# One written order for the steps of the first four pairs of heads

## The chip, the cores and the metric

The kernel runs on one core of a Trainium2 chip. The metric is the device time of one execution in microseconds (us); the time before is 978.82 us, the median of three runs (978.48 to 979.66).

## The reference

Attention over 4 batches of 8 heads with 576 positions of 64 values, in float32, then two feed-forward blocks over the 2304 tokens of 512 values:

```python
q_rot, k_rot = rotate(q), rotate(k)                   # x1*cos - x2*sin, x1*sin + x2*cos
scores = q_rot @ k_rot.T / 8
attn = exp(scores - max(scores)); attn /= attn.sum() + 1e-9
x = (attn @ v) as [2304, 512]
x = gate * relu(x @ w1[e]) @ w2[e]                    # e = the best of 8 experts, for each token
out = relu(x @ w_in) ** 2 @ w_out
```

## The kernel before

The 32 heads are worked on as 16 pairs, 0 to 15; two heads fill the 128 partitions. A pair goes through steps, each a Python function that issues a few instructions. The change names each step by a letter; this document does so throughout, so that `S1.2` is score unit 2 of pair 1:

- **L** `load`: one DMA of q and k (1280 KB) into tile `qk`, which has two buffers. **V** `load_v`: one DMA of v (320 KB) into tile `V`, two buffers. Both are issued on SP's queue.
- **R** or **Q** `rotate`: three elementwise operations (two products, one sum), in place in `qk`, on DVE (R) or on POOL (Q). The number behind the pair is 0 for k, 1 for q, empty for both; the last number says which of the three.
- **H** `high`: ACT copies `qk` rounded to fp32r into `XH`. **W** or **w** `low`: what the rounding left goes to `XL`, on POOL (W) or DVE (w). H and W are the last readers of a `qk` buffer, so the load of two pairs later waits for them.
- **Z** `stack_up`: ten DMAs inside SBUF, on SP's queue, that stack high and low parts into `kZ`, `qZ` and `QH` (four for k, six for q). Pair 0 does without them: **b**, **c** and **d** build its parts by columns on DVE and ACT, and each of its score units is followed by two warm-up matmuls.
- **S** `scores`: one of nine score units of a pair, 4 matmuls of 288 columns (6 in unit 8) into one of two PSUM buffers `ps`. **M** `smax`: the row maximum on DVE. **X** `sexp`: the exponential on ACT, which frees the buffer.
- **U** `turn`: one of eleven transposing units, four 128x128 transposes of the exponentials on TensorE (one in unit 6), into one of four PSUM buffers `pp`. **O** `turned`: the copy out, on DVE for seven units and on ACT for four.
- **A** `values`: half of the product with v, 20 short matmul instructions that need all of the pair's O and its `V`. **G** `gathered`: its copy out. **J** `project`, **F** `finish`: the projection by identity and gate weights, and the division on DVE. **K** `gate_weights`: DMAs of the gate weights and of a table of constants.

Nothing reorders instructions: each engine runs them in the order in which the functions are called, and each DMA is issued in SP's order, so that an instruction which waits holds up what is behind it on its engine. That order comes from a heap of (time, function) pairs that `at` fills and a loop at the end of `attention` empties. For each pair, `on` adds the pair's number times 15.954 to a step's offset in `OFF`. Pair 0's score units and pair 1's rotations stand in a list, `opening()`, at times 0.0, 0.1 and so on, ahead of all offsets; `FIRST` draws six of pair 0's transposing units to times 29.5 to 30.5. So pair 0's transposes are issued after its last score unit. Pair 2 has its own branch: q rotated on POOL, k on DVE. A tile's buffer passes to the next user when the last reader of its content is done, also where that reader is issued later on another engine.

After attention come routing and the experts, with weights that are loaded during attention, and a dense block; both are long runs of matmuls.

Of the kernel before, what the change touches and what calls it, by code (L numbers as in the profile page):

```python
# [21 lines left out]
B, H, S, D = 4, 8, 576, 64  # L22
# [37 lines left out]
def shape_constants():  # L60
# [27 lines left out]
    for b in range(B):  # L88
        for c in range(4):
# [21 lines left out]
           un=[32.589, 32.153, 35.217, 38.036, 36.617, 23.748, 28.906, 37.6, 35.653, 34.253, 33.817],  # L111
           out=[33.418, 34.148, 36.917, 39.025, 37.411, 29.788, 32.958, 38.405, 36.294, 35.538, 34.643],
           av=[41.194, 44.969], x=[46.747, 47.789], pj=54.426, fin=58.03)
FIRST = [(0, 1), (0, 0), (1, 3), (1, 2), (0, 2), (1, 1)]
ON_DVE = [(0, 0), (0, 3), "LQ", "CR", (1, 0), (1, 1), (1, 3)]


def attention(tc, rope, ident, qk, v, w_gate, xd, on_batch, later, ahead):
    nc = tc.nc
# [59 lines left out]
    def warm(n):  # L179
        nc.tensor.matmul(T["warm"][:, 0:n], T["hi", 0][:, 0, 0:128], T["hi", 0][:, 0, 0:n], start=True, stop=True)  # L180

    def opening():


        two = lambda s: (lambda: scores(0, s), lambda: smax(0, s), lambda: sexp(0, s))
        S, M, X = [dict(zip(range(9), [two(s)[n] for s in range(9)])) for n in range(3)]
        step = lambda n, i: lambda: rotate(1, n, nc.vector, i)
        return [S[0], S[1], lambda: rotate(0, 1, nc.vector, cols=Z), lambda: direct_high(0, Z), M[0], X[0], M[1], X[1],
                lambda: direct_low(0, nc.vector, Z), lambda: load(2), S[4], S[5], step(0, 0), M[4], X[4], step(0, 1), M[5], X[5],
                step(0, 2), S[8], S[2], M[8], X[8], lambda: high(1, 0), lambda: low(1, 0), lambda: stack_up(1, 0),  # L190
                step(1, 0), M[2], X[2], step(1, 1), S[3], S[6], M[3], X[3], step(1, 2), lambda: high(1, 1), M[6], X[6],
                lambda: low(1, 1), lambda: stack_up(1, 1), lambda: load_v(0), S[7], M[7], X[7]]
# [26 lines left out]
    def load(P):  # L219
        t = T["qk", P] = ldp.tile([128, 2, 2, 640], F32, name="qk", tag="qk", bufs=2)  # L220
        src = qk[P].rearrange("p (w n c) -> p w n c", w=2, n=2)
        if P < 2:
            for n, c in ([(0, h) for h in HALF] + [(1, A), (1, Z)] if P == 0 else [(n, slice(0, 640)) for n in range(2)]):
                nc.sync.dma_start(out=t[:, :, n, c], in_=src[:, :, n, c])
        else:
            nc.sync.dma_start(out=t, in_=src)
# [5 lines left out]
    def rotate(P, n, eng, step=None, cols=slice(0, 640)):  # L232
        x, a = T["qk", P], slice(0, 2) if n is None else slice(n, n + 1)
        for i, (f, o, y) in enumerate(((times, 0, TB[:, 0, a, cols]), (times, 1, TB[:, 1, a, cols]), (plus, 0, x[:, 1, a, cols]))):
            if step in (None, i):
                f(eng, x[:, o, a, cols], x[:, o, a, cols], y)

    def high(P, n=None, cols=slice(0, 640)):

        if ("hi", P) not in T:  # L240
            T["hi", P] = zp.tile([128, 2, 640], F32R, name="XH", tag="XH", bufs=2)
        a = slice(0, 2) if n is None else slice(n, n + 1)
        nc.scalar.activation(T["hi", P][:, a, cols], T["qk", P][:, 0, a, cols], AF.Copy)

    def low(P, n=None, eng=None):
        if ("lo", P) not in T:
            T["lo", P] = zp.tile([128, 2, 640], F32R, name="XL", tag="XL", bufs=2)
        a = slice(0, 2) if n is None else slice(n, n + 1)
        args = T["lo", P][:, a], T["qk", P][:, 0, a], T["hi", P][:, a].bitcast(F32)
        if eng is None:  # L250
            nc.gpsimd.tensor_sub(*args)
        else:
            minus(eng, *args)
# [16 lines left out]
    def scores(P, s):  # L270

        t = T["S", P, s] = ps.tile([128, 2, 512], F32, name="ps", tag="ps", bufs=2)
        if s < 8:
            j, c = divmod(s, 4)
            todo, qs, qh = [j], slice(c * 128, c * 128 + 128), QH[P % 2][j]
            qh = qh[:, qs]
        else:
            todo, qs, qh = [0, 1], slice(512, 640), T["hi", P][:, 1, 512:640]
        k0 = 0 if s in (4, 5, 6, 7) else 64
        if P == 0:  # L280
            H, L = T["hi", P], T["lo", P]
            ql = L[:, 1, 512:640] if s == 8 else T["qZ", 2 * P + j][:, qs]
            for i, (q1, k1) in enumerate(((qh, H), (ql, H), (qh, L))):
                for u in range(2):
                    nc.tensor.matmul(t[:, u, 0:288], q1, k1[:, 0, k0 + 288 * u:k0 + 288 * u + 288], start=i == 0, stop=i == 2)
            for u in range(2):
                warm(288)
            return
        for i, j in enumerate(todo):
            Q1, K1 = T["qZ", 2 * P + j], T["kZ", 2 * P + j]  # L290
            for u in range(2):
                nc.tensor.matmul(t[:, u, 0:288], Q1[:, qs], K1[:, k0 + 288 * u:k0 + 288 * u + 288], start=i == 0, stop=False)  # L292
        for u in range(2):
            nc.tensor.matmul(t[:, u, 0:288], qh, T["lo", P][:, 0, k0 + 288 * u:k0 + 288 * u + 288], start=False, stop=True)  # L294
# [6 lines left out]
    def smax(P, s):  # L301
        nc.vector.tensor_reduce(small("mx", P, 9)[:, s:s + 1], T["S", P, s][:, :, 0:288], axis=AX.XY, op=ALU.max, negate=True)  # L302

    def sexp(P, s):
        if ("e", P) not in T:
            T["e", P] = (wp.tile([128, 4, 1152], F32, name="e", tag="e", bufs=2), wp.tile([128, 576], F32, name="e4", tag="e4", bufs=2))
        ed = T["e", P][1] if s == 8 else T["e", P][0][:, s % 4, 576 * (s // 4):576 * (s // 4) + 576]
        sc = s if s < 4 else (4 if s == 8 else s + 1)
        nc.scalar.activation(ed.rearrange("p (u n) -> p u n", u=2), T["S", P, s][:, :, 0:288], AF.Exp,  # L309
                             bias=T["mx", P][:, s:s + 1], accum_out=SS[P % 6][:, sc, 0:1])  # L310
# [87 lines left out]
            at(t, lambda: route(P, t))  # L398

    prepare()  # L400
    for n, f in enumerate(opening()):
        at(.1 * n, f)
    at(24.0, gate_weights)
    for P in range(NPAIR):
        def on(o, f, *args):
            at(OFF["pair"] * P + o, lambda: f(*args))

        if P > 2:
            on(OFF["load"], load, P)
        if P > 0:  # L410
            on(OFF["v"] + (1.8 if P == NPAIR - 1 else 0), load_v, P)
        if P > 1:
            for i in range(3):
                if P == 2:
                    on(OFF["rope"] + 2.93 * i, rotate, P, 1, nc.gpsimd, i)
                    on(1.1 + 1.35 * i, rotate, P, 0, nc.vector, i)
                else:
                    on(OFF["rope"] + 2.93 * i, rotate, P, None, nc.gpsimd, i)
            for n, hi, lo in ((1, 1.6, 1.7), (0, 4.7, 4.75)) if P == 2 else ((None, OFF["hi"], OFF["lo"]),):
                on(hi, high, P, n)  # L420
                on(lo, low, P, n)
            on(OFF["z"], stack_up, P)
        for s in range(9) if P else ():
            w = {1: 8, 8: 1}.get(s, s) if P == 1 else s
            on(OFF["S"][w], scores, P, s)
            on(OFF["max"][w], smax, P, s)
            on(OFF["exp"][w], sexp, P, s)
        for un, o, o2 in zip(UNITS, OFF["un"], OFF["out"]):
            if P == 0 and un in FIRST:
                o, o2 = [t + .2 * FIRST.index(un) for t in (29.5, 29.6)]  # L430
            on(o, turn, P, un)
            on(o2, turned, P, un)
        for u in range(2):
            on(OFF["av"][u], values, P, u)
            on(OFF["x"][u], gathered, P, u)
        on(OFF["pj"], project, P)
        on(OFF["fin"], finish, P)
        if P % 4 == 3 and P + 1 < NPAIR:
            on(OFF["fin"] + .02, route, P)
    at(OFF["pair"] * (NPAIR - 1) + OFF["lo"] + .01, swap.close)  # L440
    at(OFF["pair"] * (NPAIR - 1) + max(OFF["S"]) + .01, turned_in.close)
    ahead(lambda t, f: at(t, f), lambda: ppt("pp"))
# [845 lines left out]
```

## Time and profile before

| | |
|---|---|
| median of three runs | 978.82 us |
| the profiled execution | 982.82 us, its span 981.0 us |
| TensorE matmul (PE) busy | 961.1 us, 98% of the span |
| VectorE (DVE) / ScalarE (ACT) / GpSimd (POOL) busy | 55% / 43% / 33% |
| mean granted TensorE clock | 0.994 of 2.4 GHz |

The profile is one execution; its times count from the start of the span, and the other 1.8 us of the profiled execution lie around it. PE is the matmul engine, PEld its weight loads, SPq the queue on which SP issues DMAs. A clock of 0.50 in a row is the lower of TensorE's two levels, 1.2 GHz.

### The profile page before, as it was taken

Reading aid. Unit: us, or ns where it says so; the run is one execution under the profiler, and the core shown is the slowest. Engines: PE = TensorE matmul, PEld = TensorE weight load, DVE = VectorE, ACT = ScalarE, POOL = GpSimd, SP = SyncE. Lnnn points to the kernel's source line nnn. Section 1 sums busy time; section 2 is a strip of 40 time slices with the busy share of each in tenths; the row PEclk is TensorE's granted clock in tenths of the full one; section 3 lists DMA queues with packets and bytes.
Section 4 is the critical chain, followed back from the end, with each engine's and each line's share of the span. In section 5 each row is a group of like instructions: output and inputs, shape, how many; then the busy total and the mean of one; then the engine's idle time right before and its main releaser. Section 6 shows DMA issues by size and latency. Waiting matters only on the chain. (4 is left out here: it accounts for less than half of the span.)

```text
span 981.0 us, 15523 instructions
## 1 busy us (share of the span) xinstructions
PE 961.1 (98%) x5565; PEld 825.5 (84%) x5565; DVE 537.5 (55%) x949; ACT 422.3 (43%) x840; POOL 320.1 (33%) x261
## 2 busy tenths in 40 slices
PE   8899999999999999999999999999999999999997
PEld 7687878788787888888888789999999999999996
DVE  7677877777867355574685479522323323222222
ACT  5576757575641233352464367522322322222222
POOL 3776887887475221142354300010000100100101
PEclk9899999999999999999999999999999999999999
DMA  6876777766632823455486423100100200100000
GB/s 210 257 201 194 230 214 188 247 186 164 184 110 89 313 97 130 131 182 176 160 277 229 165 90 129 33 33 1 33 33 1 65 1 31 35 1 1 33 1 33
DMA packets 46353, 119.83 MB, mean 122 GB/s; under 512 B 8240, under 2 KB 9776, under 8 KB 43952
## 3 DMA queue, kind: packets, MB, share of 16 engines
q1 hardware_dynamic: 40752, 101.58, 33.6%
q0 software_dynamic: 4960, 16.43, 4.9%
q8 instruction: 46, 0.75, 0.3%
q10 hardware_dynamic: 544, 0.66, 0.2%
q14 instruction: 51, 0.42, 0.1%
HBM read 79.93 MB, written 15.11 MB: 97 GB/s over the span
## 5 line engine op out<-in xcount | busy, mean ns | idle before, releaser
L1114 PE MATMUL o<-Wo,gs 128*128 128x512 f32 x864 | 214.7, 393 | 0.0
L1093 PE MATMUL h<-xs,Wi 128*128 128x384 f32 x1008 | 189.6, 336 | 0.0
L1114 PEld LDWEIGHTS o<-Wo,gs 128*128 128x128 f32 x864 | 159.9, 188 | 28.7 <-DVE gs L1104 0.3
L1093 PEld LDWEIGHTS h<-xs,Wi 128*128 128x128 f32 x1008 | 178.2, 188 | 6.6
L1102 DVE SCALAR_TENSOR_TENSOR g<-h,r 128x384 f32<-128x384 f32 x80 | 44.6, 558 | 190.6 <-ACT r L1098 190.6
L309 ACT ACTIVATE e<-ps,mx 128x576 f32<-128x576 f32 x144 | 106.2, 740 | 86.8 <-DVE mx L302 86.7
L1129 POOL DMA_INDIRECT out_dram<-os,at x18 | 17.8, 987 | 369.3 <-DVE os L1124 309.9
L1098 ACT ACTIVATE r<-h 128x384 f32<-128x384 f32 x96 | 47.1, 490 | 204.6 <-PE h L1093 204.6
L302 DVE TENSOR_REDUCE mx<-ps 128x1 f32<-128x576 f32 x144 | 105.9, 753 | 53.0 <-PE ps L294 53.0
L916 PE MATMUL p_y<-W,hh 128*128 128x512 f32 x504 | 122.9, 399 | 0.8 <-ACTq L928 0.8
L887 PE MATMUL p_h<-W,xs 128*128 128x512 f32 x480 | 114.9, 394 | 0.0
L916 PEld LDWEIGHTS p_y<-W,hh 128*128 128x128 f32 x504 | 93.1, 188 | 22.2 <-ACTq L928 1.1
L887 PEld LDWEIGHTS p_h<-W,xs 128*128 128x128 f32 x480 | 88.5, 188 | 18.4 <-DVEq L928 0.7
L327 PE MATMUL pp<-ident,e 128*128 128x128 f32 x640 | 87.0, 277 | 1.6 <-DVE eT L343 1.3
L1104 DVE TENSOR_TENSOR gs<-g,gs 128x384 fp32r<-128x384 f32 x96 | 53.6, 558 | 56.0 <-ACT gs L1103 56.0
L459 POOL TENSOR_TENSOR qk<-qk,TB 128x1280 f32<-128x1280 f32 (+1 forms) x28 | 78.6, 2824 | 2.2 <-DMA qk<-in_qk_dram 2.2
L327 PEld LDWEIGHTS pp<-ident,e 128*128 128x128 f32 x640 | 75.7, 143 | 3.2 <-DVE eT L343 1.8
L292 PE MATMUL ps<-kZ,qZ 128*128 128x288 f32 x300 | 72.1, 330 | 3.9 <-ACT e L309 3.0
L1103 ACT ACTIVATE gs<-g 128x384 fp32r<-128x384 f32 x96 | 50.4, 525 | 50.5 <-DVE g L1102 50.0
L354 PE MATMUL av<-eT,V 128*64 128x288 f32 x512 | 69.1, 412 | 0.0
L343 DVE COPY eT<-pp 128x512 f32<-128x512 f32 x96 | 64.3, 684 | 5.8 <-PE pp L327 4.0
L292 PEld LDWEIGHTS ps<-kZ,qZ 128*128 128x128 f32 x300 | 45.8, 192 | 19.3 <-issue 6.7
(237 smaller groups left out, 1206.0 us busy)
## 6 DMA issues: line engine op xcount, KB each, us to landing
qk<-in_qk_dram SPq DMA_DIRECT2D x14, 1280.0 KB, 6.4
raw<-in_moe_w_dram SPq DMA_DIRECT2D x30, 512.0 KB, 5.5
kZ<-XH SPq DMA_DIRECT2D x60, 160.0 KB, 2.8
rawa<-in_moe_w_dram SPq DMA_DIRECT2D x18, 512.0 KB, 3.7
w<-in_moe_w_in_dram SPq DMA_DIRECT2D x8, 1024.0 KB, 6.0
w<-in_moe_w_out_dram SPq DMA_DIRECT2D x8, 1024.0 KB, 5.0
V<-in_v_dram SPq DMA_DIRECT2D x16, 320.0 KB, 3.0
qZ<-XH SPq DMA_DIRECT2D x30, 160.0 KB, 2.9
```

What stands on the lines that cost most here:

```text
L292: nc.tensor.matmul(t[:, u, 0:288], Q1[:, qs], K1[:, k0 + 288 * u:k0 + 288 * u + 288], start=i == 0, stop=False)
L302: nc.vector.tensor_reduce(small("mx", P, 9)[:, s:s + 1], T["S", P, s][:, :, 0:288], axis=AX.XY, op=ALU.max, negate=True)
L309: nc.scalar.activation(ed.rearrange("p (u n) -> p u n", u=2), T["S", P, s][:, :, 0:288], AF.Exp, bias=T["mx", P][:, s:s + 1], accum_out=SS ...
L327: nc.tensor.transpose(t[:, c * 128:c * 128 + 128], src, ident)
L343: nc.vector.tensor_copy(o, i)
L354: nc.tensor.matmul(t[64 * j:64 * j + 64], V[:, j, kc], eT[:, j, kc, cs] if kc < 4 else eL[:, cs], start=kc == 0, stop=kc == 4)
L459: v.tensor_tensor(out=out, in0=a, in1=b, op=ALU.mult)
L887: nc.tensor.matmul(t[u], s[:, a, k], W1[:, b, k, 512 * u:512 * u + 512], start=n == 0, stop=n == 11)
L916: nc.tensor.matmul(t, s[:, a, k], W2[:, b, k], start=n == 0, stop=n == 23)
L1093: nc.tensor.matmul(t, W[:, a, k, fs], s[:, c, k], start=n == 0, stop=n == 11)
L1104: nc.vector.tensor_sub(gs[:, 1], g, gs[:, 0].bitcast(F32))
L1114: nc.tensor.matmul(self.T["o", b][c], gs[:, a, 128 * c:128 * c + 128], W[:, w], start=(f == 0 and n == 0), stop=(f == 15 and n == 2))
```

## The change

`opening()` and `FIRST` go. In their place a string `ORDER` gives 228 steps of pairs 0 to 3, with the loads and preparation of pair 4, one after the other; step n stands at time 75.70 n / 228 on the same heap. `do` turns a token into its call. A token in `ORDER` is left out of the loop over pairs; all others keep their offsets, so steps of pairs 4 to 6 whose offset is below 75.70 fall between the written ones: `L5`, `L6`, `V4` and `Q5..0` to `Q5..2`. Behind the written stretch the heap gives out the same steps in the same order as before.

In the order that results, pair 0's transposes stand between score units of pairs 0 and 1. One low part of pair 1 is made on DVE (`w1.1`); two of pair 2's q rotations go to DVE and two of its k rotations to POOL. `K` comes early, ahead of `L2`. Around `V2` the heap gives, with pair 5's and 6's steps by their times: `H4 S3.4 ... X3.4 ... S3.1 ... Q5..0 S3.0 J1 M3.0 U2.7 L6 X3.1 X3.0 S3.5 W4 V2 Q5..1 S3.7 V4 O2.9 O2.7 Z4 M3.5 A2.0`; before, `V2` stood between `L4` and `Z3`, and `W4` ahead of `Q5..0`, `Z4` and `L6`.

```diff
--- before.py
+++ after.py
@@ -111,7 +111,17 @@
            un=[32.589, 32.153, 35.217, 38.036, 36.617, 23.748, 28.906, 37.6, 35.653, 34.253, 33.817],
            out=[33.418, 34.148, 36.917, 39.025, 37.411, 29.788, 32.958, 38.405, 36.294, 35.538, 34.643],
            av=[41.194, 44.969], x=[46.747, 47.789], pj=54.426, fin=58.03)
-FIRST = [(0, 1), (0, 0), (1, 3), (1, 2), (0, 2), (1, 1)]
+UNTIL = 75.70
+ORDER = """
+    b S0.1 M0.1 c S0.0 X0.1 d M0.0 R1.0.0 S0.4 M0.4 X0.0 S0.5 R1.0.1 M0.5 X0.4 S0.8 R1.0.2 X0.5 M0.8 K S0.2 H1.0 R1.1.0 X0.8 R1.1.1 L2 R1.1.2 S0.3 M0.2
+    H1.1 X0.2 M0.3 U0.6 w1.1 X0.3 U0.5 S0.7 W1.0 R2.1.0 M0.7 S0.6 Z1.0 Q2.1.1 U0.2 Z1.1 M0.6 R2.0.0 U0.1 X0.7 L3 S1.2 O0.2 X0.6 R2.1.2 O0.1 S1.1 M1.2 M1.1
+    U0.7 O0.6 U0.3 O0.3 X1.2 X1.1 S1.4 M1.4 U0.0 H2.1 Q2.0.1 O0.7 S1.8 Q2.0.2 M1.8 W2.1 X1.4 H2.0 O0.5 U0.10 S1.0 M1.0 X1.8 O0.0 U0.9 U0.4 S1.5 M1.5 U1.5
+    O0.4 X1.0 X1.5 O0.10 U0.8 S1.6 U1.6 O0.8 O0.9 W2.0 Q3..0 V0 S1.7 M1.6 M1.7 O1.5 Z2 X1.6 A0.0 Q3..1 Q3..2 S2.2 X1.7 U1.10 O1.6 U1.9 G0.0 U1.7 O1.9 M2.2
+    X2.2 O1.10 S1.3 M1.3 X1.3 L4 H3 A0.1 S2.8 S2.4 O1.7 U1.0 V1 M2.8 M2.4 U1.1 G0.1 X2.8 O1.0 W3 X2.4 U1.8 U1.2 O1.8 S2.1 O1.2 U1.3 Q4..0 M2.1 S2.0 J0
+    O1.1 U1.4 X2.1 O1.3 M2.0 X2.0 U2.5 O1.4 S2.7 Z3 S2.5 O2.5 M2.7 X2.7 A1.0 M2.5 F0 S2.3 X2.5 S2.6 M2.3 M2.6 X2.3 X2.6 Q4..1 A1.1 G1.1 S3.2 Q4..2 U2.1
+    M3.2 S3.8 U2.6 G1.0 M3.8 U2.0 O2.0 O2.1 X3.2 U2.3 H4 S3.4 O2.6 U2.2 X3.8 U2.4 U2.10 M3.4 O2.3 S3.1 O2.4 X3.4 U2.8 O2.2 U2.9 O2.10 M3.1 O2.8 S3.0 J1
+    M3.0 U2.7 X3.1 X3.0 S3.5 W4 V2 S3.7 O2.9 O2.7 Z4 M3.5 A2.0 M3.7 U3.5 X3.5 F1 X3.7 V3
+""".split()
 ON_DVE = [(0, 0), (0, 3), "LQ", "CR", (1, 0), (1, 1), (1, 3)]
 
 
@@ -179,17 +189,20 @@
     def warm(n):
         nc.tensor.matmul(T["warm"][:, 0:n], T["hi", 0][:, 0, 0:128], T["hi", 0][:, 0, 0:n], start=True, stop=True)
 
-    def opening():
-
-
-        two = lambda s: (lambda: scores(0, s), lambda: smax(0, s), lambda: sexp(0, s))
-        S, M, X = [dict(zip(range(9), [two(s)[n] for s in range(9)])) for n in range(3)]
-        step = lambda n, i: lambda: rotate(1, n, nc.vector, i)
-        return [S[0], S[1], lambda: rotate(0, 1, nc.vector, cols=Z), lambda: direct_high(0, Z), M[0], X[0], M[1], X[1],
-                lambda: direct_low(0, nc.vector, Z), lambda: load(2), S[4], S[5], step(0, 0), M[4], X[4], step(0, 1), M[5], X[5],
-                step(0, 2), S[8], S[2], M[8], X[8], lambda: high(1, 0), lambda: low(1, 0), lambda: stack_up(1, 0),
-                step(1, 0), M[2], X[2], step(1, 1), S[3], S[6], M[3], X[3], step(1, 2), lambda: high(1, 1), M[6], X[6],
-                lambda: low(1, 1), lambda: stack_up(1, 1), lambda: load_v(0), S[7], M[7], X[7]]
+    def do(token):
+        k, a = token[0], [int(i) if i else None for i in token[1:].split(".")] if token[1:] else []
+        if k in "SMXAG":
+            dict(S=scores, M=smax, X=sexp, A=values, G=gathered)[k](*a)
+        elif k in "UO":
+            (turn if k == "U" else turned)(a[0], UNITS[a[1]])
+        elif k in "RQ":
+            rotate(a[0], a[1], nc.vector if k == "R" else nc.gpsimd, a[2])
+        elif k in "Ww":
+            low(a[0], a[1] if a[1:] else None, None if k == "W" else nc.vector)
+        elif k in "bcd":
+            dict(b=lambda: rotate(0, 1, nc.vector, cols=Z), c=lambda: direct_high(0, Z), d=lambda: direct_low(0, nc.vector, Z))[k]()
+        else:
+            dict(H=high, Z=stack_up, L=load, V=load_v, J=project, F=finish, K=gate_weights)[k](*a)
 
     def direct_high(P, cols):
 
@@ -398,45 +411,28 @@
             at(t, lambda: route(P, t))
 
     prepare()
-    for n, f in enumerate(opening()):
-        at(.1 * n, f)
-    at(24.0, gate_weights)
+    for n, token in enumerate(ORDER):
+        at(UNTIL * n / len(ORDER), lambda token=token: do(token))
     for P in range(NPAIR):
-        def on(o, f, *args):
-            at(OFF["pair"] * P + o, lambda: f(*args))
+        def on(o, token):
+            if token not in ORDER:
+                at(OFF["pair"] * P + o, lambda: do(token))
 
         if P > 2:
-            on(OFF["load"], load, P)
+            on(OFF["load"], f"L{P}")
+            for i in range(3):
+                on(OFF["rope"] + 2.93 * i, f"Q{P}..{i}")
+            for k, o in (("H", "hi"), ("W", "lo"), ("Z", "z")):
+                on(OFF[o], f"{k}{P}")
         if P > 0:
-            on(OFF["v"] + (1.8 if P == NPAIR - 1 else 0), load_v, P)
-        if P > 1:
-            for i in range(3):
-                if P == 2:
-                    on(OFF["rope"] + 2.93 * i, rotate, P, 1, nc.gpsimd, i)
-                    on(1.1 + 1.35 * i, rotate, P, 0, nc.vector, i)
-                else:
-                    on(OFF["rope"] + 2.93 * i, rotate, P, None, nc.gpsimd, i)
-            for n, hi, lo in ((1, 1.6, 1.7), (0, 4.7, 4.75)) if P == 2 else ((None, OFF["hi"], OFF["lo"]),):
-                on(hi, high, P, n)
-                on(lo, low, P, n)
-            on(OFF["z"], stack_up, P)
-        for s in range(9) if P else ():
-            w = {1: 8, 8: 1}.get(s, s) if P == 1 else s
-            on(OFF["S"][w], scores, P, s)
-            on(OFF["max"][w], smax, P, s)
-            on(OFF["exp"][w], sexp, P, s)
-        for un, o, o2 in zip(UNITS, OFF["un"], OFF["out"]):
-            if P == 0 and un in FIRST:
-                o, o2 = [t + .2 * FIRST.index(un) for t in (29.5, 29.6)]
-            on(o, turn, P, un)
-            on(o2, turned, P, un)
-        for u in range(2):
-            on(OFF["av"][u], values, P, u)
-            on(OFF["x"][u], gathered, P, u)
-        on(OFF["pj"], project, P)
-        on(OFF["fin"], finish, P)
+            on(OFF["v"] + (1.8 if P == NPAIR - 1 else 0), f"V{P}")
+        for k, o in (("S", "S"), ("M", "max"), ("X", "exp"), ("U", "un"), ("O", "out"), ("A", "av"), ("G", "x")):
+            for u, t in enumerate(OFF[o]):
+                on(t, f"{k}{P}.{u}")
+        on(OFF["pj"], f"J{P}")
+        on(OFF["fin"], f"F{P}")
         if P % 4 == 3 and P + 1 < NPAIR:
-            on(OFF["fin"] + .02, route, P)
+            at(OFF["pair"] * P + OFF["fin"] + .02, lambda P=P: route(P))
     at(OFF["pair"] * (NPAIR - 1) + OFF["lo"] + .01, swap.close)
     at(OFF["pair"] * (NPAIR - 1) + max(OFF["S"]) + .01, turned_in.close)
     ahead(lambda t, f: at(t, f), lambda: ppt("pp"))
```

## Rows read from the trace of the kernel before

**Rows 1.** The page, part 1: busy time and share of the span of TensorE's engines.

```profile
PE 961.1 (98%) x5565; PEld 825.5 (84%) x5565; DVE 537.5 (55%) x949; ACT 422.3 (43%) x840; POOL 320.1 (33%) x261
```

**Rows 2.** Windows: us, busy of PE, PEld, DVE, ACT, POOL, granted clock, DMA share, GB/s.

```profile
10.00:20.00 10.00, 7.82 (x57) 7.12 (x55) 9.84 (x18) 5.26 (x14) 0.00 (x0) 1.00 0.49 181
...
30.00:40.00 10.00, 7.04 (x34) 6.34 (x34) 8.29 (x12) 5.79 (x13) 6.62 (x4) 0.70 0.87 287
40.00:50.00 10.00, 10.00 (x74) 7.16 (x73) 4.89 (x9) 5.55 (x12) 6.28 (x4) 0.95 0.90 262
```

**Rows 3.** Timeline of PEld, steady pairs: start, us, engine, line, tiles, [idle before].

```profile
64.17 0.30 PEld L292 LDWEIGHTS ps<-kZ,qZ 128*128 128x128 f32 x2 [0.44 <-ACT X L357]
...
64.68 0.92 PEld L327 LDWEIGHTS pp<-ident,e 128*128 128x128 f32 x8
...
74.09 1.65 PEld L354 LDWEIGHTS av<-eT,V 128*64 128x64 f32 x16 [0.17 <-issue]
...
80.60 0.30 PEld L292 LDWEIGHTS ps<-kZ,qZ 128*128 128x128 f32 x2 [0.44 <-ACT X L357]
```

**Rows 4.** Timeline of all engines, pairs 0 and 1.

```profile
10.69 0.30 PEld L285 LDWEIGHTS ps<-XH,QH 128*128 128x128 f32 x2
...
11.72 0.32 PEld L285 LDWEIGHTS ps<-XH,QH 128*128 128x128 f32 x2
...
14.79 0.53 PE L285 MATMUL ps<-XH,QH 128*128 128x288 f32 x2 [1.72 <-ACT e L309]
...
21.07 1.92 POOL L251 TENSOR_TENSOR XL<-qk,XH 128x640 fp32r<-128x640 f32 x1 [14.04 <-ACT XH L243]
...
22.16 1.52 DVE L455 TENSOR_TENSOR qk<-qk 128x640 f32<-128x640 f32 x1
...
23.16 0.30 PEld L285 LDWEIGHTS ps<-XH,QH 128*128 128x128 f32 x2 [0.31 <-ACT e L309]
...
28.75 0.30 PEld L292 LDWEIGHTS ps<-kZ,qZ 128*128 128x128 f32 x2 [0.99 <-issue]
...
41.23 1.65 PEld L354 LDWEIGHTS av<-eT,V 128*64 128x64 f32 x16 [0.17 <-issue]
```

**Rows 5.** Timeline of ACT, DVE and POOL after pair 3's first score unit.

```profile
64.61 1.27 ACT L243 ACTIVATE XH<-qk 128x1280 fp32r<-128x1280 f32 x1
65.86 0.74 ACT L309 ACTIVATE e<-ps,mx 128x576 f32<-128x576 f32 x1
...
65.01 0.76 DVE L302 TENSOR_REDUCE mx<-ps 128x1 f32<-128x576 f32 x1 [1.93 <-PE ps L294]
...
65.97 2.93 POOL L251 TENSOR_TENSOR XL<-qk,XH 128x1280 fp32r<-128x1280 f32 x1 [4.74 <-ACT XH L243]
```

**Rows 6.** Timeline of SP's queue of DMAs.

```profile
29.20 0.39 SPq L226 DMA_DIRECT2D qk<-in_qk_dram  x1
29.64 0.45 SPq L230 DMA_DIRECT2D V<-in_v_dram  x1
...
47.86 0.33 SPq L230 DMA_DIRECT2D V<-in_v_dram  x1
```

**Rows 7.** DMA issues in windows at 29.6, 47.8, 43 and 56 us: last number, landing.

```profile
V<-in_v_dram SPq DMA_DIRECT2D x1, 320.0 KB, 6.9
...
V<-in_v_dram SPq DMA_DIRECT2D x1, 320.0 KB, 3.0
...
qk<-in_qk_dram SPq DMA_DIRECT2D x1, 1280.0 KB, 5.9
...
qk<-in_qk_dram SPq DMA_DIRECT2D x1, 1280.0 KB, 7.0
```

**Rows 8.** Windows of 1 us after pair 15, columns as in Rows 2.

```profile
305.00:306.00 1.00, 0.03 (x1) 0.00 (x0) 0.43 (x3) 0.21 (x1) 0.00 (x0) 1.00 0.00 0
...
307.00:308.00 1.00, 1.00 (x4) 0.82 (x3) 0.88 (x4) 0.42 (x1) 0.13 (x1) 0.57 0.00 0
...
310.00:311.00 1.00, 1.00 (x5) 0.81 (x4) 0.90 (x4) 0.00 (x0) 0.34 (x1) 0.72 0.00 0
```

## Prediction, made before the changed kernel ran

> **What bounds the kernel now.** Read the page's busy times first: TensorE is busy 98% of the span, every other engine far less [rows 1]. The windows by stage show where the missing 2% lies: from 10 to 20 us PE is busy 7.82 of 10 while DVE is busy 9.84, from 30 to 40 us PE has 7.04 and a mean clock of 0.70, and from 40 us on PE is full [rows 2]. So there are two stages. The opening is paced by DVE: a score unit needs its maximum and its exponential before its PSUM buffer is free, and DVE does rotations in between. From about 41 us PE is the bound: from pair 3's first score unit, S3.2 at 64.17, to pair 4's, S4.2 at 80.60, pass 16.43 us [rows 3], with no wait of PE over 0.5 us.
>
> The heap gives out the same steps behind the written stretch, and PE has no slack there. Therefore I ask one thing: when does S4.2 start? What it gains or loses there, the end gains or loses.
>
> Unit prices, from starts that follow one another without a wait: a score unit 0.51 (64.17 to 64.68), a transposing unit 0.46 (eight transposes load in 0.92) [rows 3]; a score unit of pair 0 with its warm-up 1.03 (10.69 to 11.72) [rows 4]; a maximum starts 0.84 after its score unit and takes 0.76, an exponential 0.74, H 1.27, W 2.93 [rows 5].
>
> **Part 1: the opening, up to S0.7.** The written order puts pair 0's transposes where PE waited, which costs nothing as long as PE waits there. But DVE's list changes too. After b and M0.1 comes d, which waits for c on ACT and ends near 15.3, as before. Then M0.0, R1.0.0, M0.4, R1.0.1, M0.5, R1.0.2, M0.8, R1.1.0 follow at 0.70 to 0.74 each, to about 21.1. H1.0 on ACT is done near 20.5 and POOL starts W1.0. In the trace this operation took 1.92 beside DVE's rotations where others like it take 1.54, and the rotation that met it took 1.52 and ended 0.69 after it [rows 4]. R1.1.1 now meets it in full: W1.0 ends near 22.4, R1.1.1 at 23.1, R1.1.2 at 23.9, and only then M0.2, which stood between rotations before. X0.2 is also behind H1.1 on ACT: it runs from 24.75 and frees S0.7's buffer at 25.6. S0.7 started at 23.16 [rows 4]; now 25.65. PE has S0.3 and two transposing units (21.3 to 22.9), then idles 2.7 us. If the two engines don't meet, 1.6; I take 2.7.
>
> **Part 2: to A0.0.** S0.7, S0.6 and two transposing units (2.06 + 0.92) bring PE to 28.6. S1.2 needs six DMAs of pair 1's q, of which the third holds w1.1's result: done on DVE at 26.1, landing 2.9 later, 29.1 (before: 28.75 [rows 4]). K moved ahead of L2 issues while SP's queue is empty, so it delays nothing, and `K` no longer stands between V1 and Z2. From S1.2 to A0.0 PE now has seven score units of 0.51, one of six matmuls (0.78), eight transposing units of 0.46 and one of 0.11: 8.1 us. Each score unit still waits for the exponential two units before it, about 2.5 us after that unit's start; with transposes between, I count 1.8 us of waits (bounds 0.8 and 3). A0.0 starts at 39.0, against 41.23 [rows 4]. S1.6 and its small transposing unit are then done as well, which were behind A0.0 before: 0.6. The gain is 2.8 us. Most of it is the half-clock stretch, which goes: clock means of 0.70 and 0.95 over two slices of 10 us [rows 2] make (0.30 + 0.05) x 10 / 0.5 = 7.0 us at 1.2 GHz. From here to S3.2 PE runs full in both kernels. Bounds of the gain: 4.0 (no meeting of POOL and DVE), 1.5 (the clock falls in the new idle stretch, below).
>
> **Part 3: V2, the load that is now late.** SP issues in order. The written order has V2 behind W4, and the heap puts L6 ahead of V2. L6 writes the buffer that W4 reads last, so L6 waits for W4, and V2, which waits for nothing of its own, stands behind it. Count from S3.2. M3.2 starts at 0.84 and takes 0.76; X3.2 runs from 1.65; H4, which the order puts behind X3.2 (before it stood ahead: 64.61 and 65.86 [rows 5]), from 2.4 to 3.7; W4 from 3.75 to 6.7. L6 is issued at 6.75 and V2 0.45 to 0.55 behind it, at 7.25. A load of v alone lands in 3.0 us, but the one issued 0.44 behind a load of q and k took 6.9, and q and k alone 5.9 to 7.0 [rows 6, 7]. Here it is the second case: V2 lands at 14.15. PE meanwhile has what lay between S3.2 and A2.0, 74.09 - 64.17 = 9.92 [rows 3], less one transposing unit (U3.5, now behind A2.0), plus 0.2 of waits: A2.0 could start at 9.65. It waits 4.5 us for V2. Nothing covers this: PE runs in order, and all of A2.0 reads V. Bounds: 0.6 (V2 lands in 3.0) and 5.3. Behind A2.0 the rest is late by the same amount but not more: Z4's ten DMAs queue behind V2 and V4 and land before S4.8 asks, by about 2 us. V3 waits for A2.1 as V4 did before.
>
> The Trainium skill, "DMA: Bandwidth & Descriptors", section "Two DMAs through the same engine are not ordered", says that transfers of one queue start in order but are pipelined, so a later one may be complete while an earlier is still writing. By that V2 might pass L6 and the wait be about 0.6. The trace's 6.9 against 3.0 [rows 7] speaks against it.
>
> **Part 4: the clock.** It fell twice before the last microseconds of the trace: in the opening's idle stretch, and at 307 us, where after a slice with PE busy 0.03 the clock is 0.57 and again 0.72 three slices later, 3.4 us at half [rows 8]. An idle stretch of 1.72 at 13 us was followed by no fall [rows 4]. A wait of 4.5 us is longer than any of these, so I expect a fall. 3.4 us at half cost 1.7 if all of it is work, less what lies in the wait: 1.0 to 2.0, I take 1.5. Of the 2.7 us in part 1 I am not sure; there a fall costs 0 to 1.7, about 1.3, since waits of PE lie in it.
>
> The Trainium skill, "TensorE: Matmul & The Clock Gate", section "HAM oscillation — how this bites in real kernels", says that waits for DMAs between stretches of matmuls return the array to half rate each time. By it the fall after V2's wait is certain; the trace, with one idle stretch followed by no fall, agrees in part.
>
> **Sum.** -2.8 + 4.5 + 0.2 + 1.5 = +3.4 us. The profiled execution, 982.82 with its span of 981.0, becomes 986.2; it stands 4.0 above the median of the runs, and the shift is the same there: 978.82 + 3.4 = 982.2 us.
>
> **The rivals.**
> - *The clock holds.* The wait is there, no fall follows. For: the 1.72 us without a fall. Against: 307 us. +1.9: 980.7.
> - *The clock falls twice,* also after the idle 2.7 us before S0.7. For: a fall followed idle time of PE in the opening before. Against: it still does warm-up matmuls. +4.7: 983.5, to 985 if the first lasts 7 us.
> - *V2 passes L6* (other side). V2 lands in 3.0 us, A2.0 waits 0.6, no fall follows. For: the pages' order of writes, and that in the trace other transfers were under way too when the v load took 6.9. Against: that 6.9. -2.8 + 0.6 + 0.2 = -2.0: 976.8, and 975.7 with the larger gain of part 2. It decides if V2 lands within about 3 us of its issue; at 5 us the kernel is level.
> - *L6 is not held by W4,* because the buffers are given otherwise than I read. Then V2 is early, and the gain of part 2 remains: 976.0. For: nothing in the trace. Against: V2 at 47.86 in the trace waited for its buffer's last reader, issued later, and held SP [rows 6].
>
> **How the numbers follow.** Forecast 0.50, the clock holds 0.17, falls twice 0.17, V2 passes 0.11, L6 free 0.05. About 0.2% (2.0 us) is what a measurement can tell from no change. Forecast, with its own range 981.0 to 983.4, and the double fall are slower, the held clock mostly within 0.2%, the last two mostly faster: slower 0.66, same 0.20, faster 0.14. The range goes from 976.6 to 985.2: V2 passing with the smaller gain at the low end, the long double fall at the high one.
>
> **What would show it.** In the profile after: S0.7 near 25.6 with R1.1.1 stretched by W1.0; no half clock from 34 to 41 us; A0.0 near 39, S3.2 near 61.3; on SP L6 waiting for POOL's XL, V2 right behind it, landing near 7 us; PE waiting for the DMA of V ahead of the values of pair 2, and a clock of 0.50 after it; S4.2 near 84. Wrong if PE finds V2 landed, if the clock stays at 1.00, or if S3.2 is not near 61.

## The result and the profile after

The changed kernel takes 989.31 us (median of six runs, 987.32 to 990.85) against 979.58 of the kernel before in the same comparison (six runs, 978.48 to 979.71): a ratio of 1.0101, 95% interval 1.0088 to 1.0115. It is slower by 9.7 us; 982.2 was predicted, inside a range that ended at 985.2. The profiled execution took 988.25, its span 986.5, the mean clock was 0.991.

The busy times of the page, part 1, barely move against [rows 1]; PE still fills 98%:

```profile
PE 962.1 (98%) x5565; PEld 826.3 (84%) x5565; DVE 536.7 (54%) x950; ACT 422.9 (43%) x840; POOL 320.2 (32%) x260
```

So it has to be read stage by stage. Windows of the kernel after, columns as in [rows 2]: up to 100 us three stretches lie at half clock, where the kernel before had one, from 34 to 41 us.

```profile
10.00:20.00 10.00, 7.80 (x44) 7.12 (x42) 9.26 (x18) 5.15 (x14) 0.00 (x0) 0.83 0.65 228
20.00:30.00 10.00, 6.10 (x35) 5.54 (x34) 9.11 (x9) 3.92 (x10) 6.16 (x3) 0.80 0.49 123
30.00:40.00 10.00, 9.83 (x64) 8.96 (x63) 8.47 (x14) 7.32 (x17) 5.02 (x3) 0.85 0.61 210
...
70.00:80.00 10.00, 4.81 (x38) 4.39 (x38) 5.95 (x15) 4.53 (x12) 7.14 (x3) 0.86 0.76 226
80.00:90.00 10.00, 10.00 (x65) 6.24 (x61) 2.66 (x4) 3.14 (x7) 0.00 (x0) 0.80 0.60 136
```

A slice whose mean clock is 0.83 has 0.17 x 10 / 0.5 = 3.4 us at half. By windows of 1 us the opening holds 3.4 such us from 15 to 20 and 6.8 from 26 to 33; the stretch from 70 to 90 holds 6.8.

The opening, timeline of the kernel after (answers [rows 4]; lines of code are shifted, L455 is a product of `rotate`, L451 its sum, L264 W, L256 H, L315 M, L298 S of pair 0):

```profile
20.59 2.91 DVE L455 TENSOR_TENSOR qk<-qk,TB 128x640 f32<-128x640 f32 x2
...
20.81 2.01 POOL L264 TENSOR_TENSOR XL<-qk,XH 128x640 fp32r<-128x640 f32 x1 [13.94 <-ACT XH L256]
...
22.79 4.19 POOL L455 TENSOR_TENSOR qk<-qk,TB 128x640 f32<-128x640 f32 x2
...
23.54 2.04 DVE L451 TENSOR_TENSOR qk<-qk 128x640 f32<-128x640 f32 x1
25.50 1.41 DVE L315 TENSOR_REDUCE mx<-ps 128x1 f32<-128x576 f32 x2
25.61 0.74 ACT L256 ACTIVATE XH<-qk 128x640 fp32r<-128x640 f32 x1 [4.07 <-DVE qk L451]
...
27.16 0.50 PEld L298 LDWEIGHTS ps<-XH,QH 128*128 128x128 f32 x2 [3.93 <-ACT e L322]
...
32.66 0.42 PEld L305 LDWEIGHTS ps<-kZ,qZ 128*128 128x128 f32 x2
...
42.52 1.41 PEld L367 LDWEIGHTS av<-eT,V 128*64 128x64 f32 x14 [0.16 <-issue]
```

W1.0 meets R1.1.0 and R1.1.1 (2.91 for two, instead of two times 0.8), nearly as forecast: there R1.1.1 alone met it and ended at 23.1, here it ends at 23.5. Right behind it POOL starts two operations that the prediction doesn't count there, Q2.1.1 and Q2.0.1; R1.1.2 meets them and takes 2.04. M0.2, H1.1 and X0.2 follow from there, and S0.7 starts at 27.16 after 3.7 us of idle PE.

The loads, timeline of the kernel after (answers [rows 3, 5, 6]; SPq L239 is `load`, L243 `load_v`, L281 Z, L367 A):

```profile
57.28 14.45 SPq L239 DMA_DIRECT2D qk<-in_qk_dram  x2
...
64.36 2.93 POOL L455 TENSOR_TENSOR qk<-qk,TB 128x1280 f32<-128x1280 f32 x1 [2.05 <-DMA qk<-in_qk_dram]
...
64.55 0.30 PEld L305 LDWEIGHTS ps<-kZ,qZ 128*128 128x128 f32 x2 [0.44 <-issue]
...
67.09 1.27 ACT L256 ACTIVATE XH<-qk 128x1280 fp32r<-128x1280 f32 x1
...
68.44 2.94 POOL L264 TENSOR_TENSOR XL<-qk,XH 128x1280 fp32r<-128x1280 f32 x1 [1.14 <-ACT XH L256]
...
71.83 0.86 SPq L243 DMA_DIRECT2D V<-in_v_dram  x2
72.75 1.21 SPq L281 DMA_DIRECT2D kZ<-XH  x2
...
79.25 4.11 PE L367 MATMUL av<-eT,V 128*64 128x288 f32 x16 [5.19 <-DMA V<-in_v_dram]
...
88.53 0.30 PEld L305 LDWEIGHTS ps<-kZ,qZ 128*128 128x128 f32 x2 [0.44 <-ACT X L370]
```

The row at 57.28 holds L5 and L6: SP stands in it until W4 ends (68.44 + 2.94 = 71.38), then V2 and V4 go out, then Z4. PE starts A2.0 only at 79.25, 5.19 us idle. The DMA issues at 71 to 72.6 us (last number: us to landing) answer [rows 7]:

```profile
qk<-in_qk_dram SPq DMA_DIRECT2D x1, 1280.0 KB, 5.9
V<-in_v_dram SPq DMA_DIRECT2D x2, 320.0 KB, 7.8
```

S3.2 starts 0.4 later than in [rows 3] (64.55 against 64.17), S4.2 7.9 later (88.53 against 80.60). That is where the time goes in the profile. Behind it nothing more is lost; the fall after the idle PE at 305 us [rows 8] is even missing (windows of 1 us, as there):

```profile
305.00:306.00 1.00, 1.00 (x11) 1.00 (x10) 0.87 (x6) 0.00 (x1) 1.00 (x2) 1.00 0.02 4
307.00:308.00 1.00, 1.00 (x6) 0.82 (x5) 0.93 (x3) 0.00 (x0) 1.00 (x1) 1.00 0.31 131
```

### The profile page after: what moved, and what is told of

It is laid out like the page before. It is cut to its first block, busy times and chain, and to the rows that moved or that the text cites. A ratio compares the mean times of both kernels' runs of the same rounds, so it can differ in the third digit from the quotient of the medians.

```text
span 986.5 us, 15534 instructions
## 1 busy us (share of the span) xinstructions
PE 962.1 (98%) x5565; PEld 826.3 (84%) x5565; DVE 536.7 (54%) x950; ACT 422.9 (43%) x840; POOL 320.2 (32%) x260
## 5 line engine op out<-in xcount | busy, mean ns | idle before, releaser
L315 DVE TENSOR_REDUCE mx<-ps 128x1 f32<-128x576 f32 x144 | 105.8, 752 | 59.1 <-PE ps L307 56.6
L455 POOL TENSOR_TENSOR qk<-qk,TB 128x1280 f32<-128x1280 f32 (+1 forms) x28 | 79.8, 2865 | 2.1 <-DMA qk<-in_qk_dram 2.1
L367 PE MATMUL av<-eT,V 128*64 128x288 f32 x512 | 71.0, 421 | 5.2 <-DMA V<-in_v_dram 5.2
L367 PEld LDWEIGHTS av<-eT,V 128*64 128x64 f32 x512 | 34.8, 139 | 30.9 <-issue 11.3
```

What stands on the lines that cost most here:

```text
L367: nc.tensor.matmul(t[64 * j:64 * j + 64], V[:, j, kc], eT[:, j, kc, cs] if kc < 4 else eL[:, cs], start=kc == 0, stop=kc == 4)
L455: v.tensor_tensor(out=out, in0=a, in1=b, op=ALU.mult)
```

## The experiments

Two questions: is L6's place in SP's queue the whole of the loss at pairs 2 to 4, and what does the opening lose, and to whom? The table gathers the answers; the starts are those of PE's matmuls in each profile (up to 0.01 us behind their weight loads), the time at half clock is that ahead of A0.0, and S5.2 is used because every wait is over by then.

| kernel | S3.2 | at half before A0.0 | S3.2 to S5.2 | median of the runs |
|---|---|---|---|---|
| before | 64.18 | 6.8 | 32.9 | 979.5 to 979.8 |
| after | 64.55 | 10.2 | 40.4 | 989.31 |
| e1 V2 early | 64.84 | 10.2 | 39.3 | 987.22 |
| e2 parts swapped | 62.17 | 3.4 | 40.0 | 985.13 |
| e3 both | 61.29 | 0 | 37.2 | 983.23 |
| e4 clock held at A2.0 | 63.65 | 6.8 | 38.1 | 987.53 |
| f1 L6 behind Z4 | 62.49 | 3.4 | 32.8 | 980.90 |
| f2 f1 and parts | 62.82 | 6.8 | 32.8 | 978.33 |
| f3 f2, opening reordered | 62.18 | 3.4 | 32.8 | 977.90 |
| f4 before, L6 early | 63.21 | 0 | 34.7 | 980.29 |
| g1 f1, parts on POOL | 61.95 | 3.4 | 32.8 | 979.74 |
| g2 f3, clock held | 61.55 | 0 | 32.8 | 976.88 |

**V2 early.** V2 stands behind Z3 in `ORDER`, far ahead of L6.

```diff
-... S2.7 Z3 S2.5 ... S3.5 W4 V2 S3.7 ...
+... S2.7 Z3 V2 S2.5 ... S3.5 W4 S3.7 ...
```

> V2 moved in the written order from behind W4 to behind Z3, so that it is issued ahead of L5 and waits for nothing. Theory A (V2 held behind L6 and then landing behind it is most of the loss): no wait ahead of A2.0 (5.2 us in the profile after), no half clock after 77 us (2.4 us lost there), so -7.6: near 981.7 us. Rival B (the loss lies in the opening, and what V2's wait takes is given back later in any case): 987 us or more.

987.22 (986.33 to 987.88); ratio to before 1.0074 (1.0059 to 1.0089). Only 2.1 us came back, and the intervals of the two kernels (1.0088 to 1.0115 for the kernel after) just touch. Theory A fell in its number, not in its place. The number is rival B's; of its account, one half shows (what V2's wait took is taken again behind it), the other doesn't (the loss is not all in the opening, see f1). Timeline of PEld:

```profile
74.28 1.65 PEld L369 LDWEIGHTS av<-eT,V 128*64 128x64 f32 x16 [0.16 <-issue]
...
83.95 0.30 PEld L307 LDWEIGHTS ps<-kZ,qZ 128*128 128x128 f32 x2 [3.20 <-ACT XH L258]
```

What PE waits for from 62 to 90 us in this kernel (us in total, times, longest):

```profile
PE ps L307 <- DMA qZ<-XL: 3.4, 2, 2.7
```

A2.0 no longer waits. But S4.2 does, for Z4's DMAs, which stand behind L6 just as V2 did, and the clock falls after that wait (10 us from 80 at a mean of 0.73). V2's wait had covered these two, 3.4 us together.

**Pair 1's low parts swapped.** q's part goes to POOL first and k's to DVE in place of the other way round.

```diff
-... U0.6 w1.1 X0.3 U0.5 S0.7 W1.0 R2.1.0 ...
+... U0.6 w1.0 X0.3 U0.5 S0.7 W1.1 R2.1.0 ...
```

> w1.1 and W1.0 change engines (w1.0 on DVE, W1.1 on POOL), so that POOL has nothing to do until pair 1's rotations on DVE are through. Theory A2 (the rotations R1.1.1 and R1.1.2 were stretched by POOL's operations, and S0.7 stands behind them): both rotations take 0.8, S0.7 starts near 24 instead of 27.2, the half clock of 26 to 33 us is gone or shorter, and S3.2 comes 2 to 3.5 us earlier: near 986.5 us. Rival (DVE's list is long anyway, and S1.2 waits for Z1's DMAs): 989 us, S1.2 unchanged near 32.7.

985.13 (984.49 to 985.67), ratio 1.0053 (1.0039 to 1.0068): 4.2 less than after, more than expected. W1.1 needs H1.1, so POOL is idle while DVE rotates. Timeline of this kernel:

```profile
20.80 1.55 DVE L457 TENSOR_TENSOR qk<-qk,TB 128x640 f32<-128x640 f32 x2
...
22.39 0.82 DVE L453 TENSOR_TENSOR qk<-qk 128x640 f32<-128x640 f32 x1
...
24.13 1.55 POOL L266 TENSOR_TENSOR XL<-qk,XH 128x640 fp32r<-128x640 f32 x1 [17.44 <-ACT XH L258]
...
24.80 0.30 PEld L300 LDWEIGHTS ps<-XH,QH 128*128 128x128 f32 x2 [1.37 <-ACT e L324]
```

R1.1.0 to R1.1.2 take 2.4 in all where they took 4.95, and S0.7 starts at 24.80 after 1.13 us of idle PE in place of 3.7. The half clock of 26 to 33 us is not there in this execution.

**Both.**

```diff
-... U0.6 w1.1 ... W1.0 R2.1.0 ... Z3 S2.5 ... W4 V2 S3.7 ...
+... U0.6 w1.0 ... W1.1 R2.1.0 ... Z3 V2 S2.5 ... W4 S3.7 ...
```

> Both edits. If the two losses are independent they add: near 979 us, about the kernel before. If the clock falls move from one place to another, 981 to 983 us.

983.23 (981.27 to 984.74), ratio 1.0037 (1.0023 to 1.005). The profile has no half clock before its last microseconds, and S3.2 is the earliest of all, 61.29. What is left is PE's wait for Z4 (2.6 and 1.5 us; 37.2 us from S3.2 to S5.2, 4.3 too long). So neither account holds: the clock did not fall, and what stayed is a wait. The single gains, 2.1 and 4.2, do add: 6.1 came back.

**The clock held at A2.0.** 18 warm-up matmuls, whose result nothing uses, fill most of the wait for V2.

```diff
+            if token == "A2.0":
+                keep_warm(nc, ident, ppt("hold")[:, 0:128], 18)
```

> The kernel after with 18 warm-up matmuls of 128x128 issued on PE just ahead of A2.0, while it waits for V2 (additional work, results unused). If the half clock of 77 to 84 us comes from the wait, it is gone, A2.0 takes 2.6 us instead of 4.9 and the time falls by 2.4: near 987 us. Rival: the clock falls all the same, or the warm-up work delays A2.0: 989 to 990 us.

987.53 (984.04 to 988.38), ratio 1.0073 (1.0054 to 1.0091). From 74 to 84 us the clock is 1.00 where it was 0.66 in the kernel after, and S3.2 to S5.2 takes 38.1 in place of 40.4. The fall behind A2.0 is worth 2.3 us in the profile and 1.8 in the time, where the two intervals overlap by a little. Window of this kernel:

```profile
74.00:84.00 10.00, 8.80 (x74) 6.92 (x74) 3.69 (x12) 2.12 (x7) 2.34 (x1) 1.00 1.01 253
```

**L6 behind Z4.** One token more; V2 as written.

```diff
-... S3.7 O2.9 O2.7 Z4 M3.5 A2.0 ...
+... S3.7 O2.9 O2.7 Z4 L6 M3.5 A2.0 ...
```

> The changed kernel with one token more: L6, the load of pair 6's q and k, is written behind Z4 instead of coming from the heap ahead of V2. V2 then stands behind nothing that waits for W4, and Z4 stands behind no large load. Theory: what pairs 2 to 4 lost (7.6 us from S3.2 to S4.2 against the kernel before: the wait for V2, under it the wait for Z4, and the half clock after them) has L6's place in SP's queue as its one cause. Then no PE idle time over 0.7 us between 62 and 90 us, no half clock there, and 989.3 - 7.6 = 981.7 us (980.5 to 983). Rival: H4 behind X3.2 and W4 behind Q5..0 make Z4 late whatever stands in the queue, so that PE still waits at S4.2: 985 to 987. Second rival: L6, late by 10 us, makes pair 6's q and k late; then a wait shows near S6.2 and the time is 983 to 985.

980.90 (978.81 to 982.89), ratio 1.0004 (0.9989 to 1.0019): 8.4 us came back, and S3.2 to S5.2 is as long as before. Timeline:

```profile
55.23 0.59 SPq L241 DMA_DIRECT2D qk<-in_qk_dram  x1
55.93 7.00 SPq L245 DMA_DIRECT2D V<-in_v_dram  x2
...
62.49 0.30 PEld L307 LDWEIGHTS ps<-kZ,qZ 128*128 128x128 f32 x2 [0.44 <-issue]
...
66.33 1.11 SPq L283 DMA_DIRECT2D kZ<-XH  x2
...
71.94 1.65 PEld L369 LDWEIGHTS av<-eT,V 128*64 128x64 f32 x16 [0.16 <-issue]
...
74.13 0.58 SPq L241 DMA_DIRECT2D qk<-in_qk_dram  x1
...
78.84 0.30 PEld L307 LDWEIGHTS ps<-kZ,qZ 128*128 128x128 f32 x2 [0.44 <-ACT X L372]
```

V2 and V4 are issued by 62.9, Z4 starts at 66.33, L6 goes out at 74.13 in nobody's way. With L6 there, H4 behind X3.2 and W4 behind Q5..0 cost nothing (first rival), nor does L6's later start (second rival): the profile lists no wait of PE from 62 to 92 us. Moving L6 takes the whole of that loss away.

The opening of this run is that of the change, and here the clock held from 20 to 30 us. Timeline of PEld (S0.7 and S1.2) and window:

```profile
27.36 0.30 PEld L300 LDWEIGHTS ps<-XH,QH 128*128 128x128 f32 x2 [3.93 <-ACT e L324]
...
30.69 0.30 PEld L307 LDWEIGHTS ps<-kZ,qZ 128*128 128x128 f32 x2 [0.32 <-issue]
```

```profile
20.00:30.00 10.00, 5.93 (x42) 5.35 (x42) 9.71 (x11) 4.67 (x12) 6.05 (x3) 1.00 0.47 115
```

From S0.7 to S1.2 pass 3.33 us; in the kernel after, at half clock, 5.50.

**L6 behind Z4 and the parts swapped.**

```diff
-... U0.6 w1.1 ... W1.0 R2.1.0 ... O2.7 Z4 M3.5 ...
+... U0.6 w1.0 ... W1.1 R2.1.0 ... O2.7 Z4 L6 M3.5 ...
```

> The changed kernel with L6 behind Z4 and the swap of pair 1's low parts (q's part on POOL first, k's on DVE in place of the other way round: w1.0 and W1.1), which shortened the opening's gap before S0.7 and took 4.2 us off by itself. If both losses are separate: 989.3 - 7.6 - 4.2 = 977.5 us (976.5 to 979), that is 2 us below the kernel before. Rival: one half-clock stretch is counted in both figures, as the earlier pair of single edits gave 6.1 together where their single gains were 2.1 and 4.2: then 979 to 981, no faster than before.

978.33 (977.37 to 982.58), ratio 0.9986 (0.997 to 1.0001). The sum holds within 0.8; the gain over the kernel before is at the edge of what can be told.

**The opening reordered besides.**

```diff
-R1.1.0 X0.8 R1.1.1 L2 R1.1.2 S0.3 M0.2 H1.1 X0.2 M0.3 ... W1.1 R2.1.0 M0.7 ... M0.6 R2.0.0
+R1.1.0 X0.8 M0.2 X0.2 R1.1.1 L2 S0.3 R1.1.2 H1.1 M0.3 ... W1.1 M0.7 ... M0.6 R2.1.0 R2.0.0
```

> As the kernel with L6 behind Z4 and the low parts swapped, and in the opening M0.2 and X0.2 stand ahead of the rotation steps R1.1.1 and R1.1.2 and of H1.1, and R2.1.0 behind M0.6: the exponential that frees S0.7's buffer no longer waits for rotations that POOL's work stretches. Theory: S0.7 starts 1 us earlier and S1.2 is held by w1.0's DMAs as before, so 0.5 to 1.5 us less than the kernel without this: 976 to 977. Rival: what is gained at S0.7 is given back at S1.2, whose q parts come from rotations that are now 0.7 us later: no change, or 0.5 us slower.

977.90 (976.47 to 981.11), ratio 0.9975 (0.9961 to 0.999). This is faster than before, but 0.4 against the kernel without it tells nothing: S3.2 is at 62.18, as in e2 with the same time at half clock (62.17). S0.7 did come earlier (23.09; e2 has 24.80), and S3.2 did not: the rival holds.

**The kernel before with L6 early.**

```diff
-            on(OFF["load"], load, P)
+            on(OFF["load"] - (5.0 if P == 6 else 0), load, P)
```

> The kernel before, with the load of pair 6's q and k alone issued 5 us earlier on the heap: it then stands ahead of W4 and of Z4's DMAs in SP's queue, as in the changed kernel; V2 is long landed there and is not touched. Theory: the place of L6 costs only where something that is due soon stands behind it; here Z4 does, but H4 and W4 come 3 us earlier than in the changed kernel, so Z4 still lands before S4.2 asks: no change, 979.8 with 979.3 to 980.5. Rival: Z4 is held as in the changed kernel with V2 early (there PE waited 2.7 us at S4.2 and the clock fell): 982 to 985.

980.29 (978.88 to 983.47), ratio 1.0000 (0.9985 to 1.0014). The time agrees with the theory; the profile doesn't quite. What PE waits for from 62 to 90 us:

```profile
PE ps L292 <- DMA qZ<-XL: 1.5, 1, 1.5
```

S3.2 to S5.2 is 1.8 us longer than before, so Z4 was late here too. The time of the runs doesn't show these 1.8, though the profiled execution is the slowest of its twelve; that stays open. The run gave something I had not asked for: up to L6 it is the kernel before, and its opening has no half clock at all (30 to 40 us at a mean of 1.00). A0.0 starts at 39.75 in place of 41.23 [rows 4], S3.2 at 63.21 in place of 64.18. Window of this run, against the mean of 0.70 in [rows 2]:

```profile
30.00:40.00 10.00, 6.43 (x45) 5.31 (x45) 9.20 (x13) 5.69 (x13) 5.31 (x3) 1.00 0.88 287
```

**Both low parts on POOL,** on the kernel with L6 behind Z4: W1.1, which waits for R1.1.2 by way of H1.1, stands ahead of Q2.1.1 and Q2.0.1.

```diff
-... U0.6 w1.1 X0.3 U0.5 S0.7 W1.0 R2.1.0 ...
+... U0.6 W1.0 X0.3 U0.5 S0.7 W1.1 R2.1.0 ...
```

> The changed kernel with L6 behind Z4, and both low parts of pair 1 on POOL (W1.0, then W1.1 in place of w1.1). W1.1 waits for H1.1 and so for R1.1.2, and POOL's two products Q2.1.1 and Q2.0.1 stand behind it: they can no longer run beside R1.1.2, while W1.0 still meets R1.1.0 and R1.1.1. Theory: R1.1.2 took 2.04 us beside these products and takes about 0.82 without them, so that the gap of 3.7 us before S0.7 becomes 2.4 to 2.7 us. Rival: the gap stays at 3.7, because M0.2, H1.1 and X0.2 stand late in their lists whatever POOL does. The time: S1.2 waits for W1.1 and its DMAs in both cases, so within 1 us of the kernel with w1.1 (980.9).

979.74 (979.0 to 981.04), ratio 0.9999 (0.9988 to 1.0009). Timeline:

```profile
19.90 2.92 DVE L457 TENSOR_TENSOR qk<-qk,TB 128x640 f32<-128x640 f32 x2
...
20.23 1.91 POOL L266 TENSOR_TENSOR XL<-qk,XH 128x640 fp32r<-128x640 f32 x1 [13.29 <-ACT XH L258]
...
22.85 0.82 DVE L453 TENSOR_TENSOR qk<-qk 128x640 f32<-128x640 f32 x1
...
25.26 0.30 PEld L300 LDWEIGHTS ps<-XH,QH 128*128 128x128 f32 x2 [2.72 <-ACT e L324]
```

The meeting with W1.0 is unchanged (2.92), R1.1.2 is back at 0.82, and the gap is 2.5 us: what I had forecast for the change itself (2.7). The two products that POOL started early are the missing 1.2 us. The time is 1.2 below that of the kernel with `w1.1`, where less than 1 was expected; the two intervals overlap, so this tells nothing.

**The clock held in the opening,** on the kernel with all three edits.

```diff
+            if token in ("S0.4", "S1.2"):
+                keep_warm(nc, ident, T["warm"][:, 0:128], 7)
```

> The fastest kernel so far (L6 behind Z4, low parts swapped, M0.2 and X0.2 ahead of the rotations) with 7 warm-up matmuls of 128 columns ahead of S0.4 and of S1.2, where PE idles 1.87 and 1.71 us. They compute nothing that is used. Theory: the half clock of 3.4 us that follows the first of these gaps goes, and with it 0.5 to 1.7 us, less where DVE and ACT pace PE there: 976.5 to 977.5 us against 977.9. Rival: the opening is paced by DVE and by Z1's DMAs, the half clock lies in PE's slack, and nothing changes or the warm-ups cost up to 0.5: 977.9 to 978.4.

976.88 (976.49 to 978.5), ratio 0.9973 (0.9962 to 0.9984). It beats both kernels, by 2.6 us the one before. The profile shows no half clock until its last microseconds (10 to 20 and 20 to 30 us at a mean of 1.00), and the eleven runs lie within 2.0 us, those of f2 and f3 within 5.2 and 4.6. S3.2 at 61.55 against 62.18 gives 0.6 of the 1.0 us; one execution each doesn't place the rest.

## Why the prediction was wrong

Predicted shift +3.4, measured +9.7. By the prediction's own steps:

- **Part 1, the opening up to S0.7: wrong in one step.** "W1.0 ends near 22.4, R1.1.1 at 23.1, R1.1.2 at 23.9" counted one meeting of POOL and DVE and left out POOL's next two operations. A rotation is two products and a sum, and only the sum waits for both products: Q2.1.1 and Q2.0.1 needed no more than L2's data, and POOL took both at once. S0.7 came at 27.16 and not at 25.65. The gap is 1.0 longer than forecast, 3.7 us, and the run with both parts on POOL has 2.5 without this meeting; and PE reached the gap 0.6 later, at 23.46, behind the half clock of 15 to 20 us, which the prediction doesn't have.
- **Part 2, "The gain is 2.8 us. Most of it is the half-clock stretch, which goes": the step that failed.** S3.2 was to come at 61.3 and came at 64.55, a loss of 0.4; even the bound with a fall, a gain of 1.5, was missed. The half clock did not go. A0.0 came 3.5 later than forecast (42.52 against 39.0): 1.5 of this had arisen at S0.7, and 2.0 arose from S0.7 to S1.2, 5.50 us where 3.45 were counted, in the second half-clock stretch; f1 took 3.33 there at full clock. The four profiles with the opening as changed have 10.2, 10.2, 6.8 and 3.4 us at half, and S3.2 moves with them: 64.55, 64.84, 63.65, 62.49. Ahead of S3.2 these differ in the place of one load of v at most; each 3.4 us at half costs about 1 us. Three other runs give the same price: e2, f2 and e3 have one order up to S0.7, and from S0.4 to S0.7 pass 9.61 and 9.51 us with 3.4 at half, 8.58 without. Nor was the stretch a fixed part of the kernel before: f4's same opening ran without it, with S3.2 earlier by 1.0 us (1.5 if both are counted from S0.4, which varies by up to 0.6 from one execution to the next). I credited to the change an event of one execution. Compared at equal luck, f4 without a fall (63.21) and f1 with one (62.49, an estimated 61.4 without, at 1 us per 3.4 at half), the written opening is worth 1.8 us (1.5 from S0.4); behind its idle stretches of 1.9 and 3.7 us the clock fell in the profile after, and that gave the gain back. In the median times it gains nothing that can be told either: f1, which has it, is level with the kernel before (ratio 1.0004).
- **Part 3, V2 behind L6 behind W4: right, and near in size.** Expected 4.5 us of wait, measured 5.19: A2.0 could have started 9.5 behind S3.2 (9.65 expected), V2 let it go at 14.7 (14.15). V2 did not pass L6: its landing took 7.8 behind L6's 5.9 (median of V2 and V4). "Z4's ten DMAs ... land before S4.8 asks" held: from 62 to 92 us PE waited for nothing but V2. It held only behind V2's wait; with V2 early PE waited 3.4 us for them.
- **Part 4, the clock: fell as expected, larger.** 6.8 us at half and not 3.4, at a cost of 1.8 to 2.3 by e4, 1.5 expected. The Trainium skill, "TensorE: Matmul & The Clock Gate", section "HAM oscillation — how this bites in real kernels", has waits for DMAs followed by half rate each time. Here not each time: half rate came with V2's wait and with e1's for Z4, but not with e3's shorter one of 2.6 us. Idle time for ACT is no surer a sign: the gap of 3.7 us before S0.7 was followed by a fall in the kernel after and by none in f1.
- **Sum, "the shift is the same there": wrong.** In the profiled executions the shift is 988.25 - 982.82 = 5.4. It is 7.9 at S4.2 and still 7.78 at J15 (304.75 against 296.97); so behind pair 15 the kernel before loses 2.35 that the kernel after does not. The profiled execution of before lay 3.2 above its median, that of after 1.1 below. The opening's fall (1.0) and the wait with its fall at 305 us (2.35) would make these 3.2 and a little more. That the median run has neither is argued from this sum. The runs record only a mean clock, and it fits in part: of 35 runs of the kernel before in one comparison, the nine above 982 us have 0.992 to 0.994, as the profiled execution has, and 21 of the other 26 have 0.995 to 0.998.

Together: 3.4 + 3.2 (opening) + 1.3 (loads and clock) = 7.9 at S4.2, - 2.5 behind it (2.35 of them behind pair 15), + 4.3 from the profiled executions to the medians = 9.7. The other two rivals of the faster side (V2 passes L6, L6 not held) fell; "the clock falls twice" was the nearest, with 983.5 to 985 on a sum whose first term was too good.

What L6's place costs depends on what stands behind it and when that is due. With L6 behind Z4 (f1) V2's written place costs nothing, since SP isn't held. With V2 landed and L6 ahead of Z4, S3.2 to S5.2 is 1.8 us too long in f4, where H4 and W4 come early, and 6.4 in e1, where they come late and the clock falls; the change has V2 behind L6 as well and loses 7.5. That H4 and W4 make the difference between f4 and e1 is argued from the orders; no run moves them alone.

## What to carry to other kernels

When an order mixes written steps with steps from a heap, follow each DMA queue in the merged order and ask of every issue that waits what is due behind it; a wait that is removed may show the next one of the same cause. A half-clock stretch in one profile is an event of that execution until a second one shows it: don't book its end as a gain, and ask whether the new order idles PE in the same place. For work given to another engine, find by its operands when it can start, not where its step stands in the list.

## What the runs showed of the hardware

A short DVE operation with two inputs in SBUF that meets one of POOL ended when POOL's ended. Routing behind pair 15, kernel before (timeline), a DVE operation (`rt_im`) that takes 0.20 at 244.8 us, where it meets none:

```profile
300.35 0.20 DVE L451 TENSOR_TENSOR rt_d<-lg,rt_mx 128x40 f32<-128x40 f32 x1
300.57 2.40 POOL L818 TENSOR_TENSOR W<-rawa,W 128x1024 fp32r<-128x1024 f32 x1
300.58 2.44 DVE L534 SCALAR_TENSOR_TENSOR rt_im<-rt_d,consts 128x40 f32<-128x40 f32 x1
```

The same place in the kernel after:

```profile
306.71 2.41 POOL L814 TENSOR_TENSOR W<-rawa,W 128x1024 fp32r<-128x1024 f32 x1
307.04 0.80 DVE L403 TENSOR_REDUCE lg<-xl 128x40 f32<-128x320 f32 x1
307.88 0.20 DVE L524 TENSOR_REDUCE rt_mx<-lg 128x5 f32<-128x40 f32 x1
308.11 1.06 DVE L447 TENSOR_TENSOR rt_d<-lg,rt_mx 128x40 f32<-128x40 f32 x1
```

Both met operations end with POOL's, at 303.0 and near 309.1; the reductions, with one input, run beside it at their usual 0.80 and 0.20. Where they meet is a matter of microseconds upstream, and the longer meeting stands ahead of the idle PE at 305 us in the profile of before; that it brings this idle time is not shown. The Trainium skill, "SBUF — State Buffer", section "SBUF: two separate sides", says that the two engines share a pair of ports, for a DVE operation with two inputs in SBUF too, as an exclusive lock that whoever starts first holds for the whole instruction; these rows and R1.1.2's 2.04 (0.82 where it meets no operation of POOL) agree.
